# Two down turns in place of three in a fused Fourier-mixing and gated-GELU kernel, with product 5 taken one unit earlier

## The chip, the core and the metric

The kernel runs on one core of a Trainium2 chip. A core has TensorE for matrix products (PE, with its weight loads PEld), VectorE (DVE), ScalarE (ACT), GpSimd (POOL) and SyncE (SP), two on-chip memories (SBUF for operands, PSUM with eight banks for the sums of products) and sixteen DMA engines that move data between SBUF and the main memory (HBM). The metric is the device time of one execution in microseconds (us); less is better.

## What is computed

The input `x` has 2048 rows of 512 numbers, all in float32. It is normalised by row, and three things are added: `x` itself, a two-dimensional Fourier mixing of the normalised rows, and a gated feed-forward layer over them.

```python
xn = _layernorm(x, axis=-1)
# A: real part of DFT_seq(DFT_hidden(xn))
a = einsum("bsd,ed->bse", xn, dft_hid_re)
b = einsum("bsd,ed->bse", xn, dft_hid_im)
y = einsum("ts,bse->bte", dft_seq_re, a) - einsum("ts,bse->bte", dft_seq_im, b)
# B: gated layer, Dm = 512, Df = 1792
g = einsum("bsd,df->bsf", xn, w_gate)
u = einsum("bsd,df->bsf", xn, w_up)
h = gelu(g) * u
return x + y + einsum("bsf,fd->bsd", h, w_down)
```

## The kernel before

**Products.** A float32 operand is split into a high and a low part of a shorter format; ACT makes the high part (`split_hi`, line 316), DVE the low part (`split_lo`, line 321). Each product of two split operands takes three matmuls of 128 by 128 by 512 (`mm3`, line 332). On top of that, block products are done in the manner of Strassen and Winograd: seven products, numbered 0 to 6, in place of eight, with sums of blocks before and after.

**Stages.** The rows of the result are made in four chunks (c = 0 to 3) of the Fourier part, each of two passes over panels of the sequence matrix. Then come 28 units (n = 0 to 27), fourteen for each half of the rows; unit 2q and unit 2q + 1 are the gate and the up projection of pair q, and pairs 7 to 13 belong to the second half. Last come the down products of the gated layer, whose results are added to what the Fourier part left in HBM (`partial`).

**Plan.** Which instruction stands where is decided by a planner before the kernel is emitted (class `Plan`). Each operation is added with its engine, an estimated cost, what it follows, the SBUF slots it makes and uses and the PSUM banks it takes and holds. TensorE's operations run in the order in which they are added. `deadlines` and `spread` give every other operation a due time, worked back from its users; an operation that feeds a product is due earlier by `AHEAD` (8 us) than the product needs it. `run` then picks, engine by engine, what can start first, and among those what is due first. The result is one fixed order for each engine, kept on the chip by semaphores, each engine going through its own order strictly. There are 109 SBUF slots of 128 by 512 numbers (`SLOTS`); a slot is used again when its last user is done, a DMA among them. A first plan ends where chunk 2 begins; a second one (from `plan = Plan(first_half.clock, ...)`) has chunks 2 and 3, the units and the down products. T2 is the start of the second on the planner's clock and TU the start of the units.

**A unit.** For n from 18 on, a unit has four products of six matmuls each: 5, 6 and 3 go into bank b, 2 into bank c. Bank b is seeded by ACT with a block that an earlier unit left in HBM (`seed`, line 1699). Product 5 is added into it, ACT copies the sum out (`q6`, `copy`, line 1644), product 6 is added, ACT copies again (`w`), product 3 is added. Product 6 waits for the copy `q6`, product 3 for the copy `w`. Bank c is seeded in the same way; DVE adds the copy `w` to it (`aw`, `sums`, line 1648); then product 2 is added (it waits for `aw`) and DVE adds `q6` (`aq`). The four blocks go through `hidden`: on even units ACT puts them through GELU (line 769), on odd ones DVE multiplies them into the gate (`up_1`, line 774). `hidden_sums` makes of the four blocks of a pair seven split operands, with four sums on DVE (line 787) and seven low parts, two slots each. `order(n)` gives the order of TensorE's work in a unit: a digit is a product, `z` is product 2 of the unit before, and `d0` to `d3` are places for down products.

**Down products.** There are 28 outputs: seven products r, two halves sp of the rows, two column blocks j. Each sums over the seven pairs of its half, three matmuls for a pair. They are cut into turns by pairs (`TURNS`). In all turns but the last, `down_op` puts a down product into `todo`, from which `fill` takes them at the places `d0` to `d3`; ACT copies its bank to a slot `part` (line 1729), and POOL issues a DMA that adds the slot to `partial` (line 1734). In the last turn (`last_down`) a product starts from a bank that ACT seeds with `partial` (line 1866), which SP has loaded (line 1855), and DVE adds the results up for the output.

**Turn of a chunk.** Between the two passes of a chunk, products 1, 3 and 2 of the second pass go on in the banks of products 0, 6 and 4 of the first. Before product 3 can begin, ACT copies bank 0 out, DVE adds product 5 and then product 6 to it (lines 1105 and 1108), and ACT writes the sum back to bank 6 (line 1110).

Of the kernel before, what the change touches and what calls it, by code (L numbers as in the profile page):

```python
# [39 lines left out]
class Plan:  # L40
# [18 lines left out]
    def add(self, name, engine, cost, fn, after=(), makes=(), uses=(), due=None, mb=0, banks=(), holds=(), adds=False, begin=0., ahead=None, soon=None):  # L59
        assert name not in self.ops, name  # L60
        after = list(after)
        if engine == "p":
            if self.products:
                after.append(self.products)
            self.products = name
        self.ops[name] = dict(e=engine, cost=cost, fn=fn, after=after, makes=dict(makes), due=due, mb=mb, adds=adds, begin=begin, soon=soon, ahead=ahead or self.ahead, early=self.early, banks=tuple(banks), drains=bool(holds) and engine != "p")
        self.size.update(makes)
        for k in (*dict(makes), *uses):
            self.users.setdefault(k, set()).add(name)
        for k in (*banks, *holds):  # L70
            self.held.setdefault(k, set()).add(name)
# [42 lines left out]
        if self.shared:  # L114
            self.spread(order, then, wanted, ready, late, need)

    shared, AHEAD = False, 0.
    BANK_SLACK = .6

    def spread(self, order, then, wanted, ready, late, need):  # L120
        for n, o in self.ops.items():
            o["due"] = wanted[n]
        for n in order:
            o = self.ops[n]
            own = late if o["due"] is None else o["due"]
            if o["due"] is None and o["drains"]:
                own = max([self.ops[a]["due"] + self.ops[a]["cost"] for a in o["after"] if a in self.ops and self.ops[a]["e"] == "p"],
                          default=late) + 6
            if o["soon"] is not None:
                own = min(own, ready[n] + o["cost"] + o["soon"])  # L130
            if n in need:
                own = min(own, max(need[n] - o["cost"], ready[n] + .3))
            took = o["cost"] + (3.5 + o["mb"] * 2.6 if o["mb"] else 0)
            tail = self.TAIL[o["e"]]
            if o["e"] == "p" and self.shared:
                continue
            o["due"] = min([own] + [self.ops[c]["due"] - took - tail * (self.ops[c]["e"] != "p" or o["e"] != "p") - self.AHEAD * (self.ops[c]["e"] == "p") for c in then[n]])

    def parts(self, o):
        return round(o["mb"] / .262) * (2 if o["adds"] else 1)  # L140
# [142 lines left out]
def fnet_geglu_kernel(ctx: ExitStack, tc: tile.TileContext, x, xt, cs, dh, wgu, wd, out):  # L283
# [245 lines left out]
    z, zps = {}, {}  # L529
# [178 lines left out]
    def fetched(n, r):  # L708
        return isinstance(n, int) and n >= NP + LEAD[r]
# [7 lines left out]
    m0, xi, wi = {}, {}, {}  # L717
# [101 lines left out]
    AHEAD = 25  # L819
# [50 lines left out]
    V5, V2, V1, A5, A2, MB = .6, .333, .1, .52, .31, .262  # L870
    plan = Plan(dict(p=10.9, v=12.0, a=11.7, s=5.6, g=8.0), 18, SLOTS - 2, AHEAD)
# [102 lines left out]
    for k in range(2, L):  # L974
        n, m = seq[k]
# [36 lines left out]
    for k in range(HS):  # L1012
# [6 lines left out]
        for j, r in enumerate(((4, 5), (6, 2))):  # L1019
            if j and k in J:  # L1020
                for i in range(2):
# [6 lines left out]
                     uses=[("t", k, j)], makes={("xc", k, j): 2})  # L1028
# [312 lines left out]
    LATER_HURRY = 28  # L1341
    FETCH_AHEAD = 22
    W_AHEAD = 12
    TURNS = [[0, 1], [2, 3], [4, 5, 6]]
    BEGIN = [4, 18, 23]
    INNER_AHEAD = 2
    SUMS_AT = -1
    U1 = 2 * NP
# [5 lines left out]
    plan.ends, plan.queue, plan.flying, plan.idle, plan.frees = (getattr(first_half, n) for n in ("ends", "queue", "flying", "idle", "frees"))  # L1354
    T2 = plan.clock["p"]
    TU = T2 + MM * (2 * HS * 42 + 48 + 72)
    add, W = plan.add, 6 * MM
    begun = {}

# [92 lines left out]
    def units():  # L1452
# [168 lines left out]
        def spot(n, place):  # L1621
            return ("b2", n - 1, 4 * (place == "c")) if from_pair(n, place) else (place, n)
# [15 lines left out]
        def copy(name, n, to, src, after, banks=(), holds=(), uses=(), more=()):  # L1638
            def f():
                if banks:  # L1640
                    bank[(n, to, *more)] = ps_tile(to)
                else:
                    side[(n, to, *more)] = slot(to)
                nc.scalar.activation((bank if banks else side)[(n, to, *more)], src(), AF.Copy)  # L1644
            add((name, n, *more), "a", A5, f, after=after, makes={(to, n, *more): 1} if not banks else {}, banks=banks, holds=[*holds, *banks], uses=uses)
# [48 lines left out]
        def seed(name, n, place, r):  # L1694
            key = (place, n)

            def f():
                bank[n, place] = ps_tile(place)
                nc.scalar.activation(bank[n, place], m0[n, r], AF.Copy)
            add((name, n), "a", A5, f, after=[("p", n - 1, 6), ("lm", n, r)], banks=[key], holds=[key], uses=[("m0", n, r)])  # L1700

        todo = [("y", r, j, g) for r in (5, 3) for j in range(2) for g in range(2)]

        def late(r, j, g):
# [77 lines left out]
        def order(n):  # L1782
            if lead(n, 1):
                return "X00 X40 " + ("W12" if lead(n - 2, 1) else "z") + " X01 X41 X04 5 X05 X44 6 X06 X45 3 X03 X02 2 X46 X10 X11"
            if lead(n - 1, 1):
                return "5 Y14 Y43 6 Y15 Y42 3 Y16 2 " + "Y13" * (n < NP - 1)
            if fetched(n, 1):
                return "5 d0 6 z d1 3 d2 d3" + " 2" * (n == U1 - 1)
            if lead(n, 4):
                return "X00 X40 " + "z " * (n > 0) + "d1 X01 X41 X04 5 1 X05 d2 6 X06 X44 d0 3 X03 X02 X45 2 d3"  # L1790
            if lead(n, 0):
                return "X00 4 X01 d1 5 1 d2 X04 6 X05 d0 3 X06 d3 2 X03"
            if lead(n - 1, 4):
                return "5 Y46 1 d1 6 Y43 Y42 d2 3 d0 d3"
            if lead(n - 1, 0):
                return "4 Y02 d1 5 1 d2 6 d0 3 d3 2"
            if n == NP and lead(n - 2, 1):
                return "5 W13 W12 6 1 3"
            if fetched(n, 4):
                return "5 1 d2 6 " + "z " * (not lead(n - 2, 1)) + "d0 3 d1 d3" + " 2" * (n == U1 - 1)  # L1800
            if fetched(n, 0):
                return "4 d1 5 1 d2 6 d0 3 d3 2"
            return "0 4 d1 5 1 d2 6 d0 3 d3 2"

        for n in range(U1):
            if n in BEGIN[1:]:
                t = BEGIN.index(n) - 1
                todo.extend(("d", t, sp, r, j) for r, sp in AHEAD for j in range(2))
            wanted = -(-len(todo) // (min(b for b in (*BEGIN, U1) if b > n) - n))
            a, b, c = (spot(n, u) for u in "abc")  # L1810
            if lead(n - 1, 0):
                copy("sb", n, "b", lambda n=n: bank_of(n, "a"), [("i", n - 1, 0, 3)], banks=[b], holds=[a])
            elif fetched(n, 0):
                if fetched(n, 1):
                    hidden(n, (0, 0), [("lm", n, 1)], lambda n=n: m0[n, 1], [], [("m0", n, 1)])
                else:
                    seed("sa", n, "a", 0)
                seed("sb", n, "b", 0)
            if fetched(n, 4):
                seed("sc", n, "c", 4)  # L1820
            ready_c = [("p", n, 4), ("sc", n), ("i", n, 4, 1), ("i", n - 1, 4, 3)]
            for u in order(n).split():
                m = n - (u == "z")
                u = u.replace("z", "2")
                if u[0] == "d":
                    for _ in range((wanted - int(u[1]) + 3) // 4):
                        fill()
                elif u[0] in "XYW":
                    X(n - "XYW".index(u[0]), int(u[1]), int(u[2]))
                else:  # L1830
                    mult(m, int(u))
                    if u == "0":
                        copy("sb", n, "b", lambda n=n: bank_of(n, "a"), [("p", n, 0)], banks=[b], holds=[a])
                    elif u == "5":
                        copy("q6", n, "q6", lambda n=n: bank[n, "b"], [("p", n, 5)], holds=[b])
                    elif u == "1":
                        hidden(n, (0, 0), [("p", n, 1)], lambda n=n: bank_of(n, "a"), [a], [])
                    elif u == "6":
                        copy("w", n, "w", lambda n=n: bank[n, "b"], [("p", n, 6)], holds=[b])
                    elif u == "3":  # L1840
                        hidden(n, (1, 0), [("p", n, 3)], lambda n=n: bank[n, "b"], [b], [])
                    elif u == "2":
                        sums("aq", m, "q6", "c", [("p", m, 2), ("q6", m)], spot(m, "c"))
                        hidden(m, (0, 1), [("aq", m)], lambda m=m: side[m, "q6"], [], [("q6", m)])
            sums("aw", n, "w", "c", [("w", n)] + [x for x in ready_c if x in plan.ops], c)
            hidden(n, (1, 1), [("aw", n)], lambda n=n: side[n, "w"], [], [("w", n)])
# [127 lines left out]
```

## Time and profile before

| | |
|---|---|
| median of 3 runs | 788.26 us |
| lowest and highest | 786.9 and 789.01 us |
| the profiled execution | 788.61 us |
| its span, first to last instruction | 786.8 us |
| granted TensorE clock, mean | 1.000 |
| HBM read, written | 131.33 MB, 76.82 MB |
| ACT `part<-dn`, line 1729 | 56 instructions |
| POOL `partial<-part`, line 1734 | 56 DMAs of 256 KB |

The span is what the profile's times count from; the difference to the profiled execution's time, 1.8 us, lies around it. A busy share is that of an engine's instructions over the span. The timeline gives each instruction's start and length; two instructions of one engine can overlap, so the time that an engine needs for each is the distance from start to start. A share of DMA over 1 in a window is a full one: it is the sum over packets, some of which reach over the window's edge.

### The profile page before, as it was taken

To read this page: it belongs to the slowest core of one execution; us is meant where nothing else is said; L and a number is where in the kernel's file an instruction comes from. 1 tells how busy PE (TensorE), PEld (TensorE's weight loads), DVE (VectorE), ACT (ScalarE), POOL (GpSimd) and SP (SyncE) were. 2 spreads that over 40 slices of the span, in tenths; PEclk is the share of its full clock that TensorE was granted. 3 is DMA by queue.
4 is the path that set the end of the run, shared out by engine and by line. 5 is a ranking of instruction groups with operands and counts; after the bars stand their busy time and mean duration, and the time that the engine had idled before them with its cause. 6 is when DMAs were issued, how large, how long until landed. Compare 5 with 4: busy or idle time off the path is not lost.

```text
span 786.8 us, 11845 instructions
## 1 busy us (share of the span) xinstructions
PE 778.6 (99%) x3429; PEld 640.6 (81%) x3429; DVE 742.4 (94%) x1410; ACT 544.1 (69%) x1034; POOL 173.3 (22%) x276
## 2 busy tenths in 40 slices
PE   9999999999999999999999999999999999998998
PEld 6888888888888888788888888888888888886887
DVE  7999999999899899999999998999999989995996
ACT  6997555557545374665767667767799888887951
POOL 0120520044221141000212221432202333433000
PEclk9999999999999999999999999999999999999999
DMA  9976997879999879993654553878996999999823
GB/s 326 390 193 190 368 343 245 272 262 285 364 382 359 314 276 377 377 345 105 166 168 147 180 179 130 292 272 305 384 389 115 242 231 212 215 269 290 262 95 147
DMA packets 104498, 205.83 MB, mean 262 GB/s; under 512 B 12624, under 2 KB 21360, under 8 KB 104240
## 3 DMA queue, kind: packets, MB, share of 16 engines
q1 hardware_dynamic: 77616, 134.01, 49.4%
q0 software_dynamic: 26528, 70.80, 32.5%
q8 instruction: 27, 0.44, 0.2%
q14 instruction: 39, 0.32, 0.1%
q10 hardware_dynamic: 288, 0.26, 0.1%
HBM read 131.33 MB, written 76.82 MB: 265 GB/s over the span
## 4 chain that ended last, share of the span: by engine, by line
PE 71%; issue 16%; POOL 7%; DVE 3%; DMA 2%; ACT 1%; POOLq 0%; ACTq 0%; DVEq 0%
PE m L332 35%; PE b L332 10%; PE y L332 10%; PE dn L332 7%; POOL partial L1734 5%; PE z L332 4%; PE c L332 4%; PE a L332 1%; DMA partial<-part 1%; POOL m_park L1652 1%; POOL h_park L1751 1%; DMA xr<-xnt 1%; DVE s L774 0%; DVE w L1648 0%; DMA x<-in_x 0%
## 5 line engine op out<-in xcount | busy, mean ns | idle before, releaser
L316 ACT ACTIVATE psh<-pan 128x512 fp32r<-128x512 f32 x203 | 117.9, 625 | 72.8 <-DVE pan L609 25.3
L321 DVE TENSOR_TENSOR psl<-pan,psh 128x512 fp32r<-128x512 f32 x198 | 129.1, 681 | 0.4 <-ACT psh L316 0.3
L332 PE MATMUL m<-psh,xch 128*128 128x512 f32 x232 | 90.5, 390 | 0.1
L332 PE MATMUL m<-psl,xch 128*128 128x512 f32 x232 | 90.3, 389 | 0.0
L332 PE MATMUL m<-psh,xcl 128*128 128x512 f32 x232 | 90.3, 389 | 0.0
L1734 POOL DMA_DIRECT2D partial<-part x56 | 48.9, 885 | 108.4 <-ACT part L1729 62.4
L332 PEld LDWEIGHTS m<-psh,xch 128*128 128x128 f32 x232 | 43.5, 188 | 9.8 <-DVE m L1115 0.8
L332 PEld LDWEIGHTS m<-psh,xcl 128*128 128x128 f32 x232 | 43.6, 188 | 9.1
L332 PEld LDWEIGHTS m<-psl,xch 128*128 128x128 f32 x232 | 43.6, 188 | 8.9
L321 DVE TENSOR_TENSOR wl<-ws,wh 128x512 fp32r<-128x512 f32 (+1 forms) x56 | 37.1, 668 | 7.8 <-ACT wh L316 5.5
L1644 ACT ACTIVATE w<-b 128x512 f32<-128x512 f32 x47 | 28.1, 599 | 23.6 <-PE b L332 22.8
L316 ACT ACTIVATE hth<-s 128x512 fp32r<-128x512 f32 x56 | 34.1, 636 | 12.8 <-DVE s L787 12.1
L1644 ACT ACTIVATE q<-b 128x512 f32<-128x512 f32 x47 | 28.1, 598 | 19.7 <-PE b L332 10.6
L609 DVE TENSOR_TENSOR pan<-pan 128x512 f32<-128x512 f32 x58 | 39.0, 681 | 2.2 <-DMA pan<-in_cs 2.2
L332 PE MATMUL m<-psh,xa 128*128 128x512 f32 x116 | 40.4, 389 | 0.0
L321 DVE TENSOR_TENSOR htl<-s,hth 128x512 fp32r<-128x512 f32 x56 | 36.6, 685 | 2.6 <-DMA partial<-part 2.5
L1080 POOL DMA_DIRECT2D t_park<-pan x29 | 16.6, 572 | 97.2 <-DVE pan L610 88.0
L574 POOL DMA_DIRECT2D partial<-part x28 | 20.8, 787 | 77.5 <-ACT part L570 69.6
L787 DVE TENSOR_TENSOR s<-s 128x512 f32<-128x512 f32 x56 | 36.6, 685 | 0.1
L316 ACT ACTIVATE wh<-ws 128x512 fp32r<-128x512 f32 (+1 forms) x56 | 34.2, 613 | 3.1 <-DVE ws L664 3.1
L1729 ACT ACTIVATE part<-dn 128x512 f32<-128x512 f32 x56 | 32.3, 591 | 0.8 <-PE dn L332 0.8
L332 PE MATMUL dn<-hth,wh 128*128 128x512 f32 x84 | 32.7, 389 | 0.0
(790 smaller groups left out, 2443.6 us busy)
## 6 DMA issues: line engine op xcount, KB each, us to landing
pan<-in_cs SPq DMA_DIRECT2D x157, 256.0 KB, 6.4
partial<-part POOLq DMA_DIRECT2D x84, 256.0 KB, 6.6
wx<-in_wgu SPq DMA_DIRECT2D x48, 256.0 KB, 4.4
m<-m_park SPq DMA_DIRECT2D x38, 256.0 KB, 5.3
t_park<-pan POOLq DMA_DIRECT2D x29, 256.0 KB, 5.6
pan<-t_park SPq DMA_DIRECT2D x29, 256.0 KB, 6.1
h_park<-s POOLq DMA_DIRECT2D x28, 256.0 KB, 3.8
s<-h_park SPq DMA_DIRECT2D x28, 256.0 KB, 8.4
```

The lines of the kernel that those rows point to most:

```text
L316: nc.scalar.activation(t[0], src, AF.Copy, scale=float(sign))
L321: engine.tensor_sub(t[1], src, hi)
L332: nc.tensor.matmul(ps, a[u][:, sl], b[v], start=first and r == 0, stop=last and r == 2, skip_group_check=resumed)
L574: nc.gpsimd.dma_start(partial[sp, r, j], ypart.pop((r, j)), **({} if r in (0, 5, 6) else {"accum_op": OP.add}))
L609: return [lambda: nc.vector.tensor_sub(t3, b22, b12), lambda: nc.vector.tensor_sub(t1, b12, b11), lambda: (nc.vector.tensor_sub(b22, *((t1 ...
L787: nc.vector.tensor_sub(t, u, v)
L1080: plan.add(("park", i), "g", .6, lambda: nc.gpsimd.dma_start(t2_park[c, k], pan_src[i][5]), after=[("S", i, 2)], mb=MB, uses=[("r", i, b22)])
L1644: nc.scalar.activation((bank if banks else side)[(n, to, *more)], src(), AF.Copy)
L1652: add(("mp", m, r), "g", .6, lambda: nc.gpsimd.dma_start(m_park[M_PARK[r], m], side[n, to, r]), after=[ready], uses=[(to, n, r)], mb=MB)
L1729: nc.scalar.activation(part[0], tile_[0], AF.Copy)
L1734: add(("da", *key), "g", .6, lambda: nc.gpsimd.dma_start(partial[sp, r, j], part[0], accum_op=OP.add), after=[("dc", *key), *sent], uses=[ ...
L1751: add(("hp", q, blk), "g", .6, lambda: nc.gpsimd.dma_start(h_park[q, H_PLACE.index(blk)], hs[q, blk]), after=[("f", n, blk)], uses=[s], mb=MB)
```

## The change

Three things are changed in the second plan.

1. `TURNS` has two turns of three and four pairs a half, in place of three of two, two and three. The first turn's 28 down products of nine matmuls stand in units 21 to 27, four to a unit (`JOBS`); the last turn's 28 have twelve matmuls each. Before, two turns of 28 down products of six matmuls stood in units 18 to 22 and 23 to 27, six to a unit.
2. Product 5 of unit n + 1 (`n5`) stands in unit n, right behind product 6, for units 18 to 27, and product 2 stands in its own unit, behind product 3. Bank b of a unit is seeded after product 5 of the unit before (it was product 6). Unit 17 makes the passage: it has product 2 of unit 16, its own product 2, and product 5 of unit 18.
3. An operation that feeds a product which the planner's clock has before TU - 20 is due 5 us ahead of it (`NEAR`) in place of 8 (`AHEAD`). In the first plan both are 0.

```diff
-    shared, AHEAD = False, 0.
+    shared, AHEAD, NEAR, FROM = False, 0., 0., 0.
...
-            o["due"] = min([own] + [self.ops[c]["due"] - took - tail * (self.ops[c]["e"] != "p" or o["e"] != "p") - self.AHEAD * (self.ops[c]["e"] == "p") for c in then[n]])
+            o["due"] = min([own] + [self.ops[c]["due"] - took - tail * (self.ops[c]["e"] != "p" or o["e"] != "p") - (self.ops[c]["e"] == "p" and (self.AHEAD if wanted[c] > self.FROM else self.NEAR)) for c in then[n]])
...
-    TURNS = [[0, 1], [2, 3], [4, 5, 6]]
-    BEGIN = [4, 18, 23]
+    TURNS = [[0, 1, 2], [3, 4, 5, 6]]
+    JOBS = ((21, 28, 0, (0, 1)),)
...
+    plan.FROM, plan.NEAR = TU - 20, 5
...
-            add((name, n), "a", A5, f, after=[("p", n - 1, 6), ("lm", n, r)], banks=[key], holds=[key], uses=[("m0", n, r)])
-
+            add((name, n), "a", A5, f, after=[("p", n - 1, 5 if place == "b" and fetched(n, 1) else 6), ("lm", n, r)], banks=[key], holds=[key], uses=[("m0", n, r)])
+
+        until = 4
...
             if fetched(n, 1):
-                return "5 d0 6 z d1 3 d2 d3" + " 2" * (n == U1 - 1)
+                return "6 " + "n5 " * (n < U1 - 1) + "d0 3 d1 2 d2 d3"
+            if fetched(n + 1, 1) and n < U1 - 1:
+                return "5 1 d2 6 z n5 d0 3 2 d1 d3"
...
         for n in range(U1):
-            if n in BEGIN[1:]:
-                t = BEGIN.index(n) - 1
-                todo.extend(("d", t, sp, r, j) for r, sp in AHEAD for j in range(2))
-            wanted = -(-len(todo) // (min(b for b in (*BEGIN, U1) if b > n) - n))
+            for first, last, t, halves in JOBS:
+                if n == first:
+                    until = last
+                    todo.extend(("d", t, sp, r, j) for r, sp in AHEAD if sp in halves for j in range(2))
+            wanted = -(-len(todo) // max(1, until - n))
...
-                m = n - (u == "z")
-                u = u.replace("z", "2")
+                m = n - (u == "z") + (u[0] == "n")
+                u = u.replace("z", "2").lstrip("n")
...
-                        copy("q6", n, "q6", lambda n=n: bank[n, "b"], [("p", n, 5)], holds=[b])
+                        copy("q6", m, "q6", lambda m=m: bank[m, "b"], [("p", m, 5)], holds=[spot(m, "b")])
```

## The prediction

> **What bounds the kernel now.** I read the page first: span and busy time by engine.
>
> ```profile
> span 786.8 us, 11845 instructions
> ## 1 busy us (share of the span) xinstructions
> PE 778.6 (99%) x3429; PEld 640.6 (81%) x3429; DVE 742.4 (94%) x1410; ACT 544.1 (69%) x1034; POOL 173.3 (22%) x276
> ```
>
> TensorE is busy for nearly all of the span and VectorE (DVE) stands close behind it. The change adds and removes no matmul, so it can win only time in which TensorE waits, and lose only by new waits. The view of waits, for PE alone, names them, longest first (total, times, longest):
>
> ```profile
> PE b L332 <- ACT q L1644: 1.8, 1, 1.8
> PE m L332 <- ACT m L1110: 1.0, 1, 1.0
> PE dn L332 <- DVE s L774: 0.8, 1, 0.8
> ```
>
> The timeline of PE shows what each really costs, from start to start (start, duration, then the instruction; idle before it in brackets):
>
> ```profile
> 332.11 0.39 PE L332 MATMUL m<-psh,xf11l 128*128 128x512 f32 x1
> 333.46 0.50 PE L332 MATMUL m<-psh,xf11h 128*128 128x512 f32 x1 [0.96 <-ACT m L1110]
> ...
> 713.18 0.39 PE L332 MATMUL dn<-htl,wh 128*128 128x512 f32 x1
> 715.37 0.50 PE L332 MATMUL b<-xT60h,wh 128*128 128x512 f32 x1 [1.80 <-ACT q L1644]
> 715.71 0.40 PE L332 MATMUL b<-xT60l,wh 128*128 128x512 f32 x1
> ...
> 722.11 0.39 PE L332 MATMUL dn<-htl,w 128*128 128x512 f32 x1
> 723.34 0.73 PE L332 MATMUL dn<-hth,w 128*128 128x512 f32 x2 [0.84 <-DVE s L774]
> ```
>
> The undisturbed step is 252.32 - 252.09 = 0.23 us (rows of the third part; 0.227 over many). So the three places lose 1.12, 1.96 and 1.00 us, and after a wait the next step is 0.34 in place of 0.23 (715.37 to 715.71), 0.11 more: 4.1 + 0.3 = 4.4 us in all, and 0.1 from 630 to 660 (29.88 us busy of 30, below). These 4.5 us are about the most that can be won, 0.6% of the time. The later two, 2.96 + 0.22 = 3.2 us, lie where down products run, the first, 1.2 us, at a turn of a chunk. Windows of the last part, one row a stretch:
>
> ```profile
> core 0: us, PE busy (x) PEld busy (x) DVE busy (x) ACT busy (x) POOL busy (x), PEclk, DMA share, GB/s
> 563.00:590.00 27.00, 27.00 (x121) 22.36 (x120) 25.66 (x54) 23.19 (x49) 2.71 (x5) 1.00 1.04 392
> 590.00:604.00 14.00, 14.00 (x64) 11.58 (x63) 13.64 (x27) 13.02 (x26) 3.52 (x4) 1.00 0.52 92
> 604.00:630.00 26.00, 26.00 (x116) 21.54 (x115) 25.81 (x49) 22.08 (x44) 9.61 (x11) 1.00 1.04 229
> 630.00:660.00 30.00, 29.88 (x132) 24.33 (x130) 27.53 (x57) 26.44 (x54) 10.93 (x13) 1.00 1.04 224
> 660.00:690.00 30.00, 30.00 (x133) 24.70 (x132) 30.00 (x54) 25.14 (x52) 11.07 (x14) 1.00 1.01 218
> 690.00:726.00 36.00, 33.36 (x146) 26.85 (x145) 26.23 (x49) 28.55 (x57) 12.87 (x15) 1.00 1.09 277
> 726.00:745.00 19.00, 19.00 (x85) 15.74 (x84) 18.53 (x31) 18.70 (x38) 0.86 (x1) 1.00 0.86 263
> 745.00:765.00 20.00, 20.00 (x90) 16.56 (x89) 19.96 (x35) 11.23 (x22) 0.00 (x0) 1.00 0.37 122
> 765.00:787.00 22.00, 18.59 (x91) 15.57 (x89) 14.28 (x23) 4.36 (x8) 0.00 (x0) 0.98 0.37 138
> ```
>
> Only 690 to 726 has fewer matmuls than its length allows (146 where 36/0.227 = 159; the trace misses a few). There DVE idles for 10 us of 36 too, and the DMA engines are full from 604 to 726. What ScalarE (ACT) waits for in 590 to 726, and the operations of the down turns (duration min/median/max, first and last start):
>
> ```profile
> ACT q L1644 <- DMA partial<-part: 6.5, 2, 4.5
> ```
>
> ```profile
> L1729 ACT ACTIVATE part<-dn x56: 575/589/624, 594.0 to 725.4; 128x512 f32<-128x512 f32 x56
> L1734 POOL DMA_DIRECT2D partial<-part x56: 858/872/1196, 595.0 to 727.3; - x56
> ```
>
> The reader is to see a chain of four links: the accumulating DMA of a down product lands late; the SBUF slot of its `part` is the one that the copy of bank b (`q`, L1644) is to write; ACT runs in order, so it stands still behind this copy, 4.5 us once; product 6 waits for the copy, and DVE, without its high parts, comes late with the multiplication that frees a bank (L774).
>
> **The change part by part.** *Two turns.* Before, each of the 28 outputs is summed in three pieces (6, 6 and 9 matmuls), afterwards in two (9 and 12). 28 evacuations go (28 x 0.589 = 16.5 us of ACT) and 28 accumulating DMAs (28 x 0.872 = 24.4 us of POOL). Neither engine is the bound, so this alone is worth nothing. The transfers are another matter; DMA queues from 650 to 690:
>
> ```profile
> q0 software_dynamic: 2271, 4.13, 64.7%
> q1 hardware_dynamic: 2930, 4.56, 35.4%
> ...
> partial<-part POOLq DMA_DIRECT2D x18, 256.0 KB, 6.1
> ```
>
> POOL's queue carries the accumulations alone: 0.647 x 40 / 18 = 1.44 us of all 16 engines for each, so 28 x 1.44 = 40 us of DMA time go from a stretch of some 130 us that is full. They still come at one in about 3.4 us (four in a unit of 60 matmuls, 13.6 us) against one in 2.3 (six in 13.6): 42% of the engines in place of 64. With the loads' 35%, squeezed by a stretch 19 us shorter, that is about 83%. So the late landing goes, and with it the waits at 715 and 723 and the little one before them: -3.3 us if all do, 0 if none; I take -3.2, since both follow from it, in a unit whose cover also grows. The last of them passes on to the next late thing, an up multiplication, which DVE then reaches in order.
>
> The Trainium skill, "Perfetto Trace Analysis", Identifying the Most-Contended Engine, speaks against this: DMA is to be judged by HBM utilization, not by occupancy of the 16 engines. By that rule 218 GB/s in 660 to 690 against 392 in 563 to 590 is no bound, and the term would be 0; it is a rival below.
>
> *Product 5 one unit earlier.* Products move, none is added. Product 6 gets 12 matmuls (2.7 us) or more behind the copy that it needs, where one or two down products stood before. Product 3 keeps six between it and its copy `w`; product 2 stands in its own unit and needs DVE's `aw` sum 12 matmuls after product 6: a copy (0.6) and a sum (0.7), so 1.4 us to spare. Queued behind such a wait would be all of PE. I cost it at 0; with no spare it would be that of the same cover in units 14 to 17, which ran 121 matmuls in 27 us, none lost.
>
> *Units 18 to 20 without down products.* The first turn now starts at unit 21, so three units of 24 matmuls (5.4 us) follow each other with nothing between. DVE's steps, from two stretches of its timeline:
>
> ```profile
> 320.05 2.49 DVE L321 TENSOR_TENSOR psl<-pan,psh 128x512 fp32r<-128x512 f32 x4
> 322.46 0.69 DVE L616 TENSOR_TENSOR pan<-pan 128x512 f32<-128x512 f32 x1
> ```
>
> ```profile
> 570.33 0.43 DVE L664 TENSOR_TENSOR ws<-ws,wx 128x256 f32<-128x256 f32 x1
> 570.67 0.42 DVE L664 TENSOR_TENSOR ws<-wx 128x256 f32<-128x256 f32 x1
> ```
>
> A full width takes 2.41 / 4 = 0.60 us from start to start, a half width 0.34. A unit needs four half sums, two half and one full low part, two sums and on average two multiplications: 6 x 0.34 + 5 x 0.60 = 5.0 of 5.4 us. By 604 two more units have passed than before, 10 us more for DVE, which had 41 - 39.3 = 1.7 idle from 563 to 604; against it the operands of the first turn are due 18 us later, of which this row stands in the same stretch:
>
> ```profile
> L321 DVE TENSOR_TENSOR hl<-s,hh 128x512 fp32r<-128x512 f32 x10 | 6.7, 683 | 0.0
> ```
>
> 10.0 - 1.7 - 6.7 = 1.6 us short at worst, 0 if operands in hand cover it. I take +0.4, a quarter. Their loads come earlier as well; the engines were at 0.52 from 590 to 604, which is room.
>
> *A longer last turn.* 336 matmuls (76.2 us) in place of 252 (57.1). DVE has for it, by code: 11 full operations for each pair (seven low parts, four sums) and 4 x 0.34 + 3 x 0.60 + 0.34 = 3.5 us for each weight, and 28 additions at the end. Before 6 x 6.6 + 3 x 3.5 + 16.8 = 67 us, 10 more than PE's time; now 8 x 6.6 + 4 x 3.5 + 16.8 = 84, 7.4 more. That much must be done ahead. Before, DVE was busy for 52.8 us after 726 (18.53 + 19.96 + 14.28), so 14 were done ahead. Bounds: 0 and +7.4; I take +0.2, near 0, by these 14.
>
> *Due 5 us ahead in place of 8.* By the code it holds for every product before the units, fourth chunk included. It moves work that DVE does in any case; loads and splits may come up to 3 us later. The smallest lead that I found there:
>
> ```profile
> 248.88 1.29 DVE L321 TENSOR_TENSOR psl<-pan,psh 128x512 fp32r<-128x512 f32 x2
> ```
>
> ```profile
> 252.09 0.39 PE L332 MATMUL m<-psh,xf13h 128*128 128x512 f32 x1
> 252.32 0.39 PE L332 MATMUL m<-psl,xf13h 128*128 128x512 f32 x1
> ```
>
> The first of the two ends at 249.6, 2.5 us before use. Ends: -1.2 (the wait at 333 goes) and 0.5 + 1.2 = +1.7 (a lead 3 us smaller is missed by 0.5, and the second turn of a chunk waits like the first). The dues of the turn's own chain move with the rest, so nothing aims at it: -0.4.
>
> Sum: -3.2 + 0 + 0.4 + 0.2 - 0.4 = -3.0 us. The profiled execution took 788.61 (span 786.8 and 1.8 around it), so 785.6; the median of the runs is 0.35 lower, so **785.3**.
>
> **The rivals.** *The waits stay* (DMA isn't what made them, or another slot's late landing takes their place): 785.3 + 3.2 = 788.5. For it: two of three waits end with an engine, not a DMA; against: ACT's 4.5 us. *Given back earlier*: units 18 to 20 cost 1.6 and the dues +1.7: 785.3 + 1.2 + 2.1 = 788.6. For it: DVE at 96% there; against: low parts are not needed at once. *Slower*: the last turn starts with nothing in hand. Eight pairs with seven operands of two slots are 112 slots of the 109 there are; before, six took 84. Then DVE's 84 us end the kernel: 785.3 + 7.4 - 0.2 = 792.5, and it decides from less than 7.4 us done ahead, first seen where r = 5 begins, which needs two sums per pair. Against it: 14 us ahead before, and 10 us of DVE's idling in 690 to 726 gone. The Trainium skill, "TensorE: Matmul & The Clock Gate", Why this matters for your kernels, has the clock halve after an idle gap over some 3 us; here 1.80 us cost 0.11 more and the clock stayed 1.00. By it a single long gap would add an estimated 1.7 us (half of its 3.4 us window) to this rival.
>
> **How the numbers follow.** About 0.3% (2.4 us, 785.9) is what a measurement tells from no change. Forecast 0.60 (0.53 of it under 785.9), waits stay 0.10, given back 0.16, slower 0.14 (0.13 over 790.6). Faster 0.53, same 0.34, slower 0.13. The range starts where all 4.5 us are won in a run as far below the median as half of what the fastest of the runs shown lies under it (788.26 - 4.5 - 0.7 = 783.0, rounded), takes in the two rivals near 788.5, and ends at 790.0; some 0.17 is left out.
>
> **What would show it.** Waits of PE on `q` and on L774 after 600 gone; ACT without a wait on `partial<-part` over 1 us; DMA share under 0.95 from the first down product to the last turn; no PE gap in the three bare units; 28 rows of `part<-dn`; PE unbroken in the last 76 us. I am wrong if gaps of 2 us or more stand at the start of the last turn or in units 18 to 20, or if the third and fourth chunk lose more than 1.5 us.

## The result, and the profile after

| | before | after |
|---|---|---|
| median of 4 runs | 788.46 us | 783.22 us |
| lowest and highest | 786.9 and 789.01 | 782.77 and 783.33 |
| span of the profiled execution | 786.8 | 781.6 |

The ratio is 0.9936, with a 95% interval of 0.9918 to 0.9953: 5.2 us less, where 3.0 were forecast. The measured time lies just inside the stated range (783.0 to 790.0), at its lower end. The runs also agree better with each other: 0.6 us from lowest to highest, before 2.1.

The page of the changed kernel, and the view of PE's waits:

```profile
span 781.6 us, 11754 instructions
## 1 busy us (share of the span) xinstructions
PE 777.5 (99%) x3432; PEld 642.2 (82%) x3432; DVE 742.2 (95%) x1410; ACT 531.4 (68%) x1006; POOL 149.5 (19%) x248
```

```profile
engine line waited for: us in total, times, longest us
PE warm L828 <- PEq L1972: 0.8, 1, 0.8
```

The share of PE is 99% in both, so the page's first line doesn't tell the two apart. The waits do: of the kernel's own waits none is left, and the one that remains stands ahead of the first matmul. The span went down by 5.2 us and DVE's busy time by 0.2 of 742: nothing was computed faster, gaps were closed. The last part of the kernel, window by window:

```profile
core 0: us, PE busy (x) PEld busy (x) DVE busy (x) ACT busy (x) POOL busy (x), PEclk, DMA share, GB/s
590.00:604.00 14.00, 14.00 (x64) 11.59 (x62) 12.80 (x32) 12.82 (x27) 0.00 (x0) 1.00 0.62 225
604.00:630.00 26.00, 26.00 (x116) 21.56 (x115) 25.78 (x50) 21.94 (x43) 4.38 (x5) 1.00 0.47 104
630.00:660.00 30.00, 30.00 (x134) 24.82 (x134) 29.51 (x52) 22.90 (x46) 7.00 (x8) 1.00 0.76 158
660.00:690.00 30.00, 30.00 (x134) 24.86 (x133) 29.41 (x59) 24.70 (x50) 8.15 (x10) 1.00 1.00 236
690.00:726.00 36.00, 36.00 (x161) 29.81 (x160) 29.40 (x49) 29.69 (x58) 4.98 (x6) 1.00 0.80 233
```

690 to 726 has 161 matmuls where 146 stood, and DVE, idle for 10 of these 36 us before, for 6.6. The DMA engines, full from 604 to 726 before, are at 0.47 to 0.80 outside 660 to 690, where they are full still (1.00). ACT's waits of 6.5 us on `partial<-part` are gone. The operations of the down turns:

```profile
L1731 ACT ACTIVATE part<-dn x28: 579/592/604, 615.1 to 702.3; 128x512 f32<-128x512 f32 x28
```

28 in place of 56, the first at 615 in place of 594. Ahead of it stand the three units without down products.

All of the 5.2 us is thus PE's waiting, and it splits in two places: the late waits (after 600 us) and the turn of a chunk (at 333 us). The three waits whose rows the prediction shows come to 4.4 us, with the slower step behind each. Two small ones, 0.27 + 0.11 us at 335.22 (not in the prediction) and 0.28 + 0.11 at 639.60 (counted there as 0.1), bring it to 5.2.

### The profile page after: what moved, and what is told of

It is laid out like the page before. It is cut to its first block, busy times and chain, and to the rows that moved or that the text cites. A ratio compares the mean times of both kernels' runs of the same rounds, so it can differ in the third digit from the quotient of the medians.

```text
span 781.6 us, 11754 instructions
## 1 busy us (share of the span) xinstructions
PE 777.5 (99%) x3432; PEld 642.2 (82%) x3432; DVE 742.2 (95%) x1410; ACT 531.4 (68%) x1006; POOL 149.5 (19%) x248
## 4 chain that ended last, share of the span: by engine, by line
PE 99%; DMA 0%; DVE 0%; ACT 0%; issue 0%
PE m L332 35%; PE b L332 22%; PE dn L332 17%; PE y L332 10%; PE c L332 8%; PE z L332 4%; PE a L332 3%; DMA x<-in_x 0%; DVE bn L400 0%; DVE p L1915 0%; DVE xa L423 0%; ACT w L411 0%; DVE stats L402 0%; PE st L1266 0%
## 5 line engine op out<-in xcount | busy, mean ns | idle before, releaser
L1736 POOL DMA_DIRECT2D partial<-part x28 | 24.5, 896 | 110.5 <-ACT part L1731 99.5
L574 POOL DMA_DIRECT2D partial<-part x28 | 20.8, 790 | 79.0 <-ACT part L570 74.5
L1649 DVE TENSOR_TENSOR w<-c,w 128x512 f32<-128x512 f32 x40 | 27.3, 689 | 6.8 <-ACT w L1645 6.5
L332 PE MATMUL dn<-hh,wh 128*128 128x512 f32 x84 | 32.7, 389 | 0.0
```

The costliest lines, as they stand in the source:

```text
L332: nc.tensor.matmul(ps, a[u][:, sl], b[v], start=first and r == 0, stop=last and r == 2, skip_group_check=resumed)
L574: nc.gpsimd.dma_start(partial[sp, r, j], ypart.pop((r, j)), **({} if r in (0, 5, 6) else {"accum_op": OP.add}))
L1649: add((name, n, *more), "v", V5, lambda: nc.vector.tensor_add(side[(n, to, *more)], bank_of(n, c) if c == "c" else bank[(n, c, *more)], si ...
L1736: add(("da", *key), "g", .6, lambda: nc.gpsimd.dma_start(partial[sp, r, j], part[0], accum_op=OP.add), after=[("dc", *key), *sent], uses=[ ...
```

## The experiments

**Each part undone, or alone.** Four kernels. The first is the kernel before with the new due times alone:

```diff
+    plan.FROM, plan.NEAR = TU - 20, 5
-            ... - self.AHEAD * (self.ops[c]["e"] == "p") for c in then[n]])
+            ... - (self.ops[c]["e"] == "p" and (self.AHEAD if wanted[c] > self.FROM else self.NEAR)) for c in then[n]])
```

> The kernel before with the new due times alone (5 us ahead in chunks 2 and 3). Theory: the due times only shuffle the chunk stage; the waits beside the down products (1.96 and 1.00 us) stay, the wait at 333 us may or may not go: 788.46 - 0.4, that is 788.1 us, within 786.8 and 789.5. Rival: the due times cured the turn of chunk 3 by themselves, 1.12 + 0.11 + 0.27 + 0.11 = 1.6 us: 786.9 us, and no PE wait on ACT m L1110.

Measured: 786.43 us (9 runs), ratio 0.9975 (0.9965 to 0.9986), 1.8 us less than the 788.25 of the runs of the kernel before that were taken with it. Its longest waits of PE:

```profile
PE b L332 <- ACT q L1645: 1.4, 1, 1.4
PE dn L332 <- DVE s L774: 0.8, 1, 0.8
```

The wait on L1110 at the turn is gone, both late ones are there. The rival was right: the due times cure the turn. The second kernel is the changed one without them:

```diff
-    plan.FROM, plan.NEAR = TU - 20, 5
+    plan.FROM, plan.NEAR = TU - 20, 8
```

> The changed kernel with 8 us ahead everywhere. Theory: the late waits stay away, the wait at the turn of chunk 3 is back as it was (the plan of that stage does not hang on what comes later): 783.22 + 1.6 = 784.8 us. Rival: the dues are worth nothing and the wait at 333 us went for another reason: 783.2 us.

Measured: 784.88 us, ratio 0.9956 (0.9942 to 0.9969), 1.7 us above the changed kernel, as expected. The waits at the turns are back (0.4 us idle on L1110 and shorter ones at both chunks), no other. So the due times are worth 1.7 to 1.8 us with either set of turns. The third is the changed kernel with the old order of products:

```diff
-                return "6 " + "n5 " * (n < U1 - 1) + "d0 3 d1 2 d2 d3"
-            if fetched(n + 1, 1) and n < U1 - 1:
-                return "5 1 d2 6 z n5 d0 3 2 d1 d3"
+                return "5 d0 6 z d1 3 d2 d3" + " 2" * (n == U1 - 1)
...
-            ... ("p", n - 1, 5 if place == "b" and fetched(n, 1) else 6) ...
+            ... ("p", n - 1, 6) ...
```

> The changed kernel with the old order of products in units 18 to 27 (5, 6, product 2 of the unit before, 3) and bank b seeded as before. Theory: fewer accumulating transfers cured the late waits, the order does nothing: 783.2 us, under 783.9, no PE wait over 0.3 us after 560 us. Rival: the 12 matmuls between product 5 and product 6 are what hides the late copy q: 785.2 to 786.4 us, with PE waits on ACT q L1645.

Measured: 786.16 us, ratio 0.9971 (0.9958 to 0.9983), 2.9 us above the changed kernel: the rival. The PE waits, and the first of them in the timelines of PE and of ACT:

```profile
PE b L332 <- ACT q L1645: 2.6, 4, 0.7
```

```profile
590.66 0.50 PE L332 MATMUL b<-xT60h,wh 128*128 128x512 f32 x1 [0.69 <-ACT q L1645]
```

```profile
588.30 1.66 ACT L316 ACTIVATE hh<-s 128x512 fp32r<-128x512 f32 x3
590.02 0.60 ACT L1645 ACTIVATE q<-b 128x512 f32<-128x512 f32 x1
```

Where no down products stand between product 5 and product 6 they follow each other, and the copy of bank b between them takes 0.6 us and the way to it, with no cover. It costs 0.85 to 0.9 us in each of units 18, 19 and 20 (timeline of PE), and a fourth wait, 0.6 us, stands at 693. That last one is a late landing again, with two turns: ACT's copy stands 1.6 us for it.

```profile
ACT q L1645 <- DMA partial<-part: 1.6, 1, 1.6
```

With the old order two turns are thus worth 0.3 us against three (786.16 and 786.43, both with the new due times), which is within the noise. The fourth kernel keeps order and due times, and takes three turns:

```diff
-    TURNS = [[0, 1, 2], [3, 4, 5, 6]]
-    JOBS = ((21, 28, 0, (0, 1)),)
+    TURNS = [[0, 1], [2, 3], [4, 5, 6]]
+    JOBS = ((18, 23, 0, (0, 1)), (23, 28, 1, (0, 1)))
```

> The changed kernel with three turns again (56 accumulating transfers, units 18 to 22 and 23 to 27), the new order and the new dues kept. Theory: late landings are back and with them 2 to 3.3 us of waits after 600 us: 785.2 to 786.5 us. Rival: the new order hides them: 783.2 to 783.8 us although ACT still waits over 1 us on partial<-part.

Measured: 785.03 us, ratio 0.9956 (0.9942 to 0.9971), from 784.23 to 786.53. That lies between the two expectations, and so does the profile: of the late waits none is there, but one of 1.02 us on an evacuation at 596, in the first down products. With 56 accumulations the new order alone gets rid of the wait on the copy `q`. In these four kernels, all with the new due times, the order is thus worth 1.4 us with three turns (786.43 to 785.03) and 2.9 with two, and the two turns 0.3 us with the old order and 1.8 with the new one: about half of their 3.2 us comes only with both.

**Product 2 left where it was.** The changed order moves two products. This kernel moves product 5 alone:

```diff
-                return "6 " + "n5 " * (n < U1 - 1) + "d0 3 d1 2 d2 d3"
+                return "6 " + "n5 " * (n < U1 - 1) + "d0 z d1 3 d2 d3" + " 2" * (n == U1 - 1)
...
-                return "5 1 d2 6 z n5 d0 3 2 d1 d3"
+                return "5 1 d2 6 z n5 d0 3 d1 d3"
```

> The changed kernel with product 5 one unit earlier, but product 2 left in the unit after, behind product 6, as before. Theory: product 5 is what counts (its copy has 18 matmuls in place of 12 to land): 783.2 us, under 783.9. Rival: product 2 in its own unit matters as well, for its bank c is freed a unit earlier: 784.2 us or more, with PE waits on a bank.

Measured: 785.65 us, ratio 0.9970 (0.9959 to 0.9981), 2.4 us above the changed kernel. PE's waits, both among the first down products (610 and 615 us):

```profile
PE dn L332 <- ACT part L1731: 1.3, 1, 1.3
PE dn L332 <- DVE s L774: 0.8, 1, 0.8
```

Both are waits of a down product for an operation that frees a PSUM bank. Product 5 early takes the next unit's bank b early; product 2 late keeps bank c of the unit before. That the two together leave too few banks fits these rows; the count of banks itself isn't in the profile.

**Are the late waits the accumulating transfers?** The kernel before, every engine in the same order, with its 56 transfers made plain writes; it leaves the earlier pieces of those sums out of the result:

```diff
-            add(("da", *key), "g", .6, lambda: nc.gpsimd.dma_start(partial[sp, r, j], part[0], accum_op=OP.add),
+            add(("da", *key), "g", .6, lambda: nc.gpsimd.dma_start(partial[sp, r, j], part[0]),
```

> The kernel before, every engine's order the same, but the 56 transfers of the first two down turns write their slot in place of adding it to HBM (so the earlier pieces of those 28 sums are left out). Theory: the DMA engines, full with accumulations, make the copy q late; lighter transfers take away the waits after 600 us, 2.5 to 3.7 us: 784.7 to 785.8 us, and no ACT wait over 1 us on partial<-part. Rival: the copy is late by the order of ACT's work, not by the transfers: 788.3 us, waits as before.

Measured: 785.03 us, ratio 0.9964 (0.9951 to 0.9976), 3.1 us less than before, as the theory had it. Its waits of PE after the start, and its busiest window:

```profile
PE m L332 <- ACT m L1110: 0.4, 1, 0.4
```

```profile
690.00:726.00 36.00, 36.00 (x161) 29.75 (x160) 28.15 (x52) 31.18 (x61) 7.60 (x14) 1.00 0.89 311
```

All late waits are gone, a wait at the turn stays. POOL's queue of DMAs, with the same 18 transfers from 650 to 690 us, shows what became lighter (the prediction has this queue's row of the kernel before: 64.7%, and 6.1 us from issue to landing):

```profile
q0 software_dynamic: 1293, 4.19, 27.1%
...
partial<-part POOLq DMA_DIRECT2D x18, 256.0 KB, 3.0
```

That is 0.271 x 40 / 18 = 0.60 us of all 16 engines for a transfer in place of 1.44. In the order of the kernel before, the accumulations were the cause; POOL's shorter issue (7.60 / 14 = 0.54 us in place of 12.87 / 15 = 0.86) comes with it and was not told apart from the transfer itself. Then the reverse: the changed kernel, with each accumulation sent a second time to a spare place.

```diff
+    spare = dram.tile([NC // 2, 7, 2, P, CH], F32, name="spare")
...
+            def send():
+                nc.gpsimd.dma_start(partial[sp, r, j], part[0], accum_op=OP.add)
+                nc.gpsimd.dma_start(spare[sp, r, j], part[0], accum_op=OP.add)
```

> The changed kernel, the same order, but each of its 28 accumulating transfers is followed by a second one of the same slot to a spare place in HBM: 56 accumulations again. Theory A (the new order covers a late copy, as in the kernel with three turns and the new order): 783.2 to 783.9 us, ACT may wait on partial<-part over 1 us, PE does not. Theory B (the gain of the two turns is the transfers that went): PE waits on q or dn come back, 784.7 us or more.

Measured: 806.4 us, ratio 1.0234 (1.0216 to 1.0252), 23 us above the changed kernel. Theory B in kind, and far beyond it in size. ACT's longest waits after 560 us, and PE's:

```profile
ACT hth L316 <- DMA spare<-part: 12.6, 2, 8.1
ACT wh L316 <- DMA spare<-part: 12.2, 2, 6.1
```

```profile
PE b L332 <- ACT w L1646: 9.1, 2, 5.4
PE dn L332 <- ACT part L1732: 5.5, 2, 4.0
```

ACT stands up to 8 us for the landing of a second transfer, which still holds the slot that ACT is to write, and nothing behind it in its queue can pass. Kernels with three turns and the new due times have as many accumulations and lie 0.3 to 3.2 us over the changed kernel (783.55 to 786.43 against 783.22), so it is not their number alone. Here the planner does not know of the second transfers and plans their slots as free too early; that this is what adds up is argued, not shown. Some 6 of the 23 us are PE's slower steps behind its longest gaps (last section). This kernel shows how the wait arises, not what 28 accumulations cost.

**Is it the turns, or the plan?** If late landings hit only where a slot happens to be used again too soon, another plan of the same work may miss them. Four kernels ask for loads at another distance in the units: two with the changed turns and order, two with three turns, the old order and the new due times.

```diff
-    FETCH_AHEAD = 22
+    FETCH_AHEAD = 20   (26 in the second and the fourth)
```

> The changed kernel with loads asked 20 us ahead of their due time in place of 22 in the units: another plan of the same work. Theory A (two turns leave room: 28 accumulations fewer): any plan of it runs nearly free of waits, PE waits after 590 us under 0.5 us in sum, 783.2 to 784.0 us. Theory B (the late waits go or stay by the accident of a plan, whichever the turns): waits of 1 us or more in this or the next, 784.3 us or more.

> The same with 26 us. Theory A: 783.2 to 784.0 us, PE waits after 590 us under 0.5 us in sum. Theory B: 784.3 us or more in this or the one before.

> The kernel before with the new due times, loads asked 20 us ahead in the units: another plan with three turns and 56 accumulations. Theory A: waits after 590 us of 1 us or more remain, 785.0 us or more. Theory B: as likely free of them as not; free in both, this and the next, speaks against A: 783.2 to 784.0 us.

> The same with 26 us. Theory A: waits after 590 us of 1 us or more remain, 785.0 us or more. Theory B: 783.2 to 784.0 us in this or the one before.

| | median | lowest to highest, runs | ratio (95%) |
|---|---|---|---|
| two turns, 20 us | 783.16 | 782.80 to 783.47, 4 | 0.9938 (0.9923 to 0.9953) |
| two turns, 26 us | 783.04 | 782.61 to 783.22, 4 | 0.9936 (0.9921 to 0.9951) |
| three turns, 20 us | 783.80 | 783.03 to 787.42, 10 | 0.9949 (0.9936 to 0.9962) |
| three turns, 26 us | 783.55 | 782.98 to 784.62, 4 | 0.9945 (0.9930 to 0.9960) |

Theory A was right of the two turns and wrong of the three. Three turns with one more number changed come within 0.3 to 0.6 us of the changed kernel, a difference that the intervals don't tell from none. The profile of the first of them, of an execution of 783.33 us, runs through the full DMA engines without a wait:

```profile
604.00:690.00 86.00, 86.00 (x381) 71.25 (x380) 85.55 (x161) 76.37 (x150) 32.27 (x38) 1.00 1.06 225
690.00:726.00 36.00, 36.00 (x160) 29.52 (x159) 27.18 (x50) 28.80 (x56) 12.17 (x14) 1.00 1.08 274
```

No trace was kept of its longer executions (up to 787.42). What goes with two turns is steadiness. The changed kernel and the two plans beside it, twelve runs, are all within 0.9 us (782.61 to 783.47); the two of three turns, fourteen runs, spread over 4.4. Apart from the doubled accumulations, every kernel here with two turns spreads over 0.5 to 1.2 us, every one with three over 1.2 to 4.4, from 4 to 16 runs each. Why is not shown: the three turns with plain writes spread over 1.7.

**Why do the due times help?** The row normalisation of the transposed input is due at fixed times, the operands of products are not. Due 3 us later, the operands let it go first: that was the theory. To tell it from a mere shuffle, the kernel before got the normalisation due 3 us earlier, and nothing else:

```diff
-    NORM_AT, NORM_STEP = 10, 7
+    NORM_AT, NORM_STEP = 7, 7
```

> The kernel before, 8 us ahead everywhere, with the fixed due times of the row normalisation of the transposed input (DVE, lines 638 and 639) set 3 us earlier. Theory: the new dues help because normalisation, due at fixed times, then goes ahead of the operands and fills DVE's idle time between chunks 2 and 3, so that the turn of chunk 3 finds DVE with more in hand; moving the normalisation alone does the same: 786.0 to 786.9 us, no PE wait on ACT m L1110. Rival: it is the shuffle of that stage, and another shuffle leaves a wait: 787.5 to 789 us.

Measured: 784.96 us, ratio 0.9963 (0.9950 to 0.9975). PE waits on L1110 are gone from the list, as the theory had it; that the time is lower than expected comes from the late waits, which this plan misses as well, with 56 accumulations; gaps of PE of 0.3 to 0.5 us are left at 245 to 247, 411 and 556 us. The row of windows from 280 to 300 us, between chunk 2 and chunk 3, of the kernel before, of the changed one and of this:

```profile
280.00:300.00 20.00, 20.00 (x90) 16.57 (x89) 17.84 (x30) 11.42 (x22) 8.29 (x14) 1.00 1.01 336
```

```profile
280.00:300.00 20.00, 20.00 (x90) 16.57 (x89) 19.72 (x33) 12.36 (x24) 7.95 (x14) 1.00 0.98 334
```

```profile
280.00:300.00 20.00, 20.00 (x90) 16.57 (x89) 19.65 (x33) 12.48 (x23) 8.93 (x16) 1.00 1.00 339
```

DVE idles 2.2 us there before and 0.3 after: three more operations get done. DVE's waits from 200 to 340 us tell what the idle time before was, a normalisation that stood for its load:

```profile
DVE xr L638 <- DMA xr<-in_xt: 2.8, 3, 1.8
```

The changed kernel and this one have no such wait. The normalisation that stands there starts at 294.7 us before, at 289.6 in the changed kernel and at 290.4 in this one. Whether the load or DVE's own order made the difference was not told apart. What it is worth shows at the turn, in ACT's timeline before and after. The rows are splits, the copy of bank 0, and the copy back that product 3 waits for:

```profile
328.05 1.16 ACT L316 ACTIVATE psh<-pan 128x512 fp32r<-128x512 f32 x2 [1.63 <-DVE pan L616]
329.11 1.07 ACT L1103 ACTIVATE p<-m 128x512 f32<-128x512 f32 x2
...
332.80 1.20 ACT L1110 ACTIVATE m<-u 128x512 f32<-128x512 f32 x2 [0.55 <-DVE u L1108]
```

```profile
325.44 1.67 ACT L316 ACTIVATE psh<-pan 128x512 fp32r<-128x512 f32 x3 [1.58 <-DVE pan L616]
327.03 1.06 ACT L1103 ACTIVATE p<-m 128x512 f32<-128x512 f32 x2
...
330.20 1.28 ACT L1110 ACTIVATE m<-u 128x512 f32<-128x512 f32 x2 [0.56 <-DVE u L1108]
```

Both copies come 2 us or more earlier. In both kernels splits stand ahead of the first copy in ACT's queue and wait 1.6 us for a DVE sum; DVE starts that sum at 327.27 us before and at 324.67 after.

## Why the prediction was right, and where its steps were wrong

**The bound** held. Every gain is a wait of PE, and what could be won at most was seen: 4.5 us by the rows shown, 5.2 with the small ones. The change won all of it, and so came out at the end of the range where everything is won, 0.2 us above its bound. That the sum, 785.3, lies 2.1 us higher is the work of the terms below: one gain was larger than forecast, and two costs did not arise.

**Two turns, -3.2.** The late waits were rightly found, but the size came out by luck: the 3.2 us between the due times alone (786.43) and the whole change (783.22) belong to turns and order together. Two turns without the new order are worth 0.3, with it 1.8. That the accumulating transfers made the late waits is shown by the plain writes. The prediction's rival by the Trainium skill, "Perfetto Trace Analysis", Identifying the Most-Contended Engine, put this term at 0; the measurement decides against it, for at 218 to 277 GB/s these transfers cost 3.1 us. That sentence of the Trainium skill goes on to say that one must then find which DMA resource binds, and the rival left that half out. The step from the transfers to the waits was too short, though. "So the late landing goes, and with it the waits" makes a number of transfers into a wait, and that link is the plan's: with full DMA engines three plans of the kernel with three turns had no late wait over 0.4 us, and with two turns and the old order one of 0.6 us remained. In the changed kernel the DMA share is 0.76 from 604 to 690 us, where the sum had 0.83; but the sign "under 0.95" throughout failed, for it is 1.00 from 660 to 690, and PE has no wait there.

**Product 5 one unit earlier, 0.** It cost nothing, as forecast, but it won a good part of what the prediction gave to the turns. The argument used units 14 to 17, where product 1 stands between product 5 and product 6; in the bare units of the old order nothing does. Undone, the order costs 2.9 us; half undone, 2.4. It was priced only as a risk; that the bare units of the new turns need it was not seen.

**Units 18 to 20, +0.4.** Measured 0. The bound that I worked out was DVE's throughput (5.0 of 5.4 us); what bites with the old order is the latency of a copy (0.85 to 0.9 us a unit), and the new order covers that. So the term and the one above belong together: the price of bare units and its cure were both in the change.

**The last turn, +0.2.** Measured 0; PE runs on without a gap to the end, and the rival that ended slower did not come.

**Due 5 us ahead, -0.4.** Here the size was wrong, -1.7 to -1.8. I asked what the shift does within the turn's chain, where all moves alike, and did not follow what doesn't move: the operations with fixed due times. "Loads and splits may come up to 3 us later" did not hold at the second turn either: there DVE's low parts stood mostly 3 us further ahead of their product than before (row by row in both timelines, products of 309 to 331 us), and the smallest lead that the prediction feared for went from 2.5 to 2.3 us only.

The sum missed by 2.2 us: 1.3 to 1.4 are the due times, 0.6 the two costs that did not arise, and the 0.2 to 0.3 left are no more than the medians of the kernel before differ from one set of runs to the next (788.16 to 788.46). Of the rivals, "the waits stay" did not come; but the plans with three turns show that such waits come and go with the plan.

## What to carry to other kernels

In a kernel whose first engine is busy at 99%, list that engine's gaps one by one with what ended each; their sum is all that a change of order or of traffic can bring, and a share of busy time tells nothing of it. A planned order that loses a few microseconds to late transfers should be tried with one number of the planner moved before the work itself is changed: it helps to tell a cause from an accident of the plan. Here three turns with one more number changed came within 0.3 to 0.6 us of the whole change, and the two turns stand out mainly by their steadier runs.

## What was not expected of the hardware

In the kernel with doubled accumulations PE had gaps long enough to lose its clock. After 1.46 us of idle time the second step is 0.23 us again, after 5.39 us it isn't:

```profile
646.63 0.50 PE L332 MATMUL dn<-hth,wh 128*128 128x512 f32 x1 [1.46 <-ACT part L1732]
646.96 0.39 PE L332 MATMUL dn<-hth,wl 128*128 128x512 f32 x1
647.19 0.40 PE L332 MATMUL dn<-htl,wh 128*128 128x512 f32 x1
```

```profile
694.40 0.80 PE L332 MATMUL b<-xT30h,w 128*128 128x512 f32 x1 [5.39 <-ACT w L1646]
694.99 0.63 PE L332 MATMUL b<-xT30l,w 128*128 128x512 f32 x1
695.42 0.63 PE L332 MATMUL b<-xT30h,w 128*128 128x512 f32 x1
```

There the step is 0.43 us, and the window from 690 to 726 has a granted clock of 0.86. The three gaps of 3.71, 4.02 and 5.39 us are each followed by such steps, the gaps of 1.46 us and, in the kernel before, of 1.80 us by none. The Trainium skill, "TensorE: Matmul & The Clock Gate", Why this matters for your kernels, puts the border at an idle gap of about 3 us; these runs agree, between 1.80 and 3.71. The prediction's estimate for one such gap, 1.7 us, is of the right size: from 694.40 to 697.88 eight steps take 3.48 us where 8 x 0.227 = 1.8 would do, 1.7 lost; behind the gap of 4.02 us ten steps (666.60 to 670.58 us) lose another 1.7; behind the gap of 3.71 us fourteen steps are slow (712.22 to 718.31 us), 2.9 lost.
